# Attention with a woven-in GLU: the last two head groups alternate chunk by chunk, so that output projections run during the last six blocks

## Chip, cores, metric

One core of a Trainium2 chip (trn2). The metric is device time of the whole program in microseconds, the median of several executions. Every execution also reports the mean granted TensorE clock of the core (1.0 is full speed).

Profiles are of single executions, so a span in a profile differs a little from the median of the runs, and is 1.7 us shorter than the time of the same execution.

## The reference

```python
x = A_x                                    # 1 x 2048 x 640, bf16
xn = layernorm(x)
qkv = (xn @ wqkv) -> q, k, v               # 32 heads of 20
o = softmax(q k^T / sqrt(20)) v            # 2048 x 2048 scores for each head
s = o @ wo                                 # 640 x 640
h = sigmoid(xn @ w_gate) * (xn @ w_up)     # 640 x 1728
g = silu(h @ w_down)
out = x + s * g
```

## The kernel before

The 32 heads are 8 groups of 4, the 2048 queries 4 chunks of 512, so attention is 32 blocks (group g, chunk c). For each block 64 tiles of scores (128 keys x 512 queries, one head) are made by TensorE. ScalarE takes the exponential of most, VectorE of the others (an integer conversion `iv` for each tile and three passes `pb` for four tiles); TensorE multiplies with the values (PV) into one accumulator bank `oacc`. The block is then divided by its row sums: through DRAM and GpSimd for most blocks (`norm_a`, `norm_b`), on chip with transposes for the last two. All other matmuls (GLU, values, keys, projections; "M work") are items that are woven in.

The order of instructions on TensorE, ScalarE and VectorE is computed when the program is built: a loop steps a clock of its own, with assumed durations, and at each step places what is ready. Parts (`...` marks what is left out):

```python
URGENT, ROUNDS, HOLD, SLACK, LEAD, LAG, D_LAST, D_LAST_END = 0.25, 4, 0.15, 0.2, 40.0, 0.0, 20, 8
D_ORD, M_ORD, WAIT3, FALL, M_END = 1, 0, 0.4, 1, 1.5
# ... blocks in the order g * 4 + c; the projection of chunk c (8 items of 5 matmuls) needs block (7, c)
# the projection of chunk 2 also needs one extra matmul for each item, from the block divided on chip

# the last block: division on chip, and the last projection, all but group 7's part, as a "prefill"
chain = [("DVE", 0.60, e_on), ("PE", 1.52, e_tr), ("DVE", 0.75, e_scale), ("PE", 0.42, e_back), ("DVE", 0.45, e_o)]
fill = [(t4 - 2, 0.2133, lambda t4=t4, kd=kd: early(mains[t4], t4, slice(0, 512), kd))
        for t4 in range(4) for kd in range(t_l + 1)]           # 20 matmuls of 512 columns
fill += [(2, 0.07, lambda ...: early(rest[...], t4, slice(512, D), kd, t4 == 0)) ...]   # 20 of 128 columns

def tail_steps():
    for _, _, f in fill:      # what is left of the prefill
        f()
    ...                       # group 7's part (late_mm), evacuation, residual, store

total = sum(x.work for x in items + glu_items if x.need is None)
def due():                    # how much M work should be placed by now
    return total * min(1.0, progress() / (NBLK - M_END))

# one step of the issue loop, TensorE's part
if full and pv_ok:
    nxt = "PV"
elif can_f and (margin < URGENT or (...)):    # a score buffer is free and ScalarE soon runs dry
    nxt = "F"
elif ...
if nxt == "F":
    ...
    jobs = claim_act(want, ...)
    if jobs or d_new is not None:
        ...                                    # place score matmuls
    elif pv_ok:
        nxt = "PV"
    elif m_ok:
        nxt = "M"
if nxt == "M":
    ...
elif nxt is None and fill and can_fill(fill[0][0]):
    fill.pop(0)[2]()                           # place a matmul of the prefill
elif nxt == "PV":
    ...
while chain or items or glu_items or ...       # (the loop's condition)
...
tail_steps()
```

## Time and profile before

| | before |
|---|---|
| median of the first runs | 841.25 us (839.08 to 841.6) |
| span of the profile | 839.8 us |
| last exponential ends | 812.7 us |
| from there to the end (the tail) | 27.1 us |
| exponential tiles on VectorE, of 2048 | 471 |

Busy time by stretch, kernel before. The columns are the stretch and its length, then busy time and number of instructions of each engine, the granted clock, the DMA share and GB/s:

```profile
core 0: us, PE busy (x) PEld busy (x) DVE busy (x) ACT busy (x) POOL busy (x), PEclk, DMA share, GB/s
795.00:812.70 17.70, 17.26 (x160) 6.67 (x158) 17.06 (x29) 17.69 (x21) 6.08 (x7) 1.00 0.54 169
812.70:831.20 18.50, 18.41 (x114) 8.44 (x111) 10.04 (x21) 0.00 (x0) 4.08 (x5) 1.00 0.39 124
831.20:839.80 8.60, 0.00 (x0) 0.00 (x0) 4.11 (x6) 0.00 (x0) 3.82 (x3) 0.70 0.22 78
```

In attention all three engines are nearly full; in the second row ScalarE has no work and TensorE has no idle time (18.41 of 18.50 us).

The timeline of the tail, kernel before; columns are start, duration, engine, line, operation, output and inputs, and how many were merged:

```profile
808.73 3.96 ACT L80 ACTIVATE pt<-scA 128x1024 bf16<-128x1024 f32 x4
...
814.72 0.68 DVE L985 COPY on<-oacc 128x512 f32<-128x512 f32 x1
...
817.46 0.39 PE L998 MATMUL tp<-ident,onq 128*80 128x128 bf16 x4
...
818.23 0.41 DVE L1002 COPY o<-tp 80x512 bf16<-80x512 bf16 x1
...
822.66 0.31 PE L765 MATMUL bk<-wo_l,oL 80*128 80x320 bf16 x1
...
823.03 2.42 PE L976 MATMUL scA<-wo,oU 128*128 128x512 bf16 x9
...
825.38 4.60 PE L976 MATMUL bk<-wo,oU 128*128 128x512 bf16 x30
...
829.91 0.40 PE L980 MATMUL bk<-wo_l,o 80*128 80x128 bf16 x4
...
830.34 0.69 DVE L1020 SCALAR_TENSOR_TENSOR hT<-bk,wd 128x512 f32<-128x512 f32 x1 [5.02 <-PE bk L980]
```

The division of the last block (accumulator copy L985, transposes L989, L998, copy L1002) is done at 818.6 us. TensorE is then still in chunk 2's projection (L765, to 823.0). Then come the prefill (L976, 823.0 to 829.9) and the last matmuls (L980).

```profile
L1194 DVE TENSOR_SCALAR iv<-bk 128x512 int16<-128x512 f32 x471 | 318.6, 682 | 31.7 <-PE bk L860 30.2
```

### The profile page before, as it was taken

To read this page: it belongs to the slowest core of one execution; us is meant where nothing else is said; L and a number is where in the kernel's file an instruction comes from. 1 tells how busy PE (TensorE), PEld (TensorE's weight loads), DVE (VectorE), ACT (ScalarE), POOL (GpSimd) and SP (SyncE) were. 2 spreads that over 40 slices of the span, in tenths; PEclk is the share of its full clock that TensorE was granted. 3 is DMA by queue.
4 is the path that set the end of the run, shared out by engine and by line. 5 is a ranking of instruction groups with operands and counts; after the bars stand their busy time and mean duration, and the time that the engine had idled before them with its cause. 6 is when DMAs were issued, how large, how long until landed. Compare 5 with 4: busy or idle time off the path is not lost.

```text
span 839.8 us, 16932 instructions
## 1 busy us (share of the span) xinstructions
PE 788.4 (94%) x6354; PEld 278.5 (33%) x6411; DVE 765.4 (91%) x1194; ACT 796.0 (95%) x1003; POOL 77.5 (9%) x84
## 2 busy tenths in 40 slices
PE   4799999999999999999999999999999999999995
PEld 2432323333333323333333233333233322333342
DVE  7789899999899998998999999999998988999994
ACT  7799999999999999999999999999999999999970
POOL 5000000000000001000000000000000000002333
PEclk9999999999999999999999999999999999999998
DMA  5711212123222132213121232131311223111642
GB/s 154 205 51 50 60 51 49 47 57 82 72 62 63 43 85 69 68 44 82 52 61 53 68 85 67 45 92 49 109 65 46 66 71 78 28 47 57 193 147 91
DMA packets 92979, 62.21 MB, mean 74 GB/s; under 512 B 34648, under 2 KB 86408, under 8 KB 92896
## 3 DMA queue, kind: packets, MB, share of 16 engines
q1 hardware_dynamic: 92608, 60.79, 25.7%
q8 instruction: 50, 0.82, 0.4%
q10 hardware_dynamic: 288, 0.33, 0.1%
q14 instruction: 33, 0.27, 0.1%
HBM read 46.24 MB, written 12.39 MB: 70 GB/s over the span
## 4 chain that ended last, share of the span: by engine, by line
ACT 49%; PE 28%; DVE 13%; issue 6%; DMA 2%; SPq 1%; POOL 0%; POOLq 0%; ACTq 0%; DVEq 0%
ACT pt L80 44%; PE scA L860 8%; PE oacc L897 5%; DVE iv L1194 5%; PE bk L679 4%; PE bk L641 3%; ACT tnh L80 3%; DVE pb L951 2%; PE bk L765 2%; PE bk L504 2%; DVE pb L945 1%; DVE pb L948 1%; DMA ld<-on 1%; PE psk L140 1%; ACT td L80 1%
## 5 line engine op out<-in xcount | busy, mean ns | idle before, releaser
L80 ACT ACTIVATE pt<-scA 128x1024 bf16<-128x1024 f32 (+1 forms) x729 | 720.2, 1153 | 4.6 <-PE bk L860 2.9
L1194 DVE TENSOR_SCALAR iv<-bk 128x512 int16<-128x512 f32 x471 | 318.6, 682 | 31.7 <-PE bk L860 30.2
L860 PE MATMUL scA<-q,kT 32*128 32x512 bf16 x1448 | 282.6, 382 | 16.7 <-ACT pt L80 9.6
L860 PE MATMUL bk<-q,kT 32*128 32x512 bf16 x600 | 215.5, 383 | 2.0 <-DVE iv L1194 1.7
L897 PE MATMUL oacc<-pt,v 128*21 128x512 bf16 x1577 | 183.1, 382 | 0.6 <-ACT pt L80 0.3
L860 PEld LDWEIGHTS <-kT 32*128 32x128 bf16 x2048 | 88.7, 91 | 261.6 <-issue 246.8
L897 PE MATMUL oacc<-pb,v 128*21 128x512 bf16 x942 | 152.9, 382 | 1.8 <-DVE on L910 1.5
L951 DVE TENSOR_TENSOR pb<-iv,pb 128x2048 bf16<-128x2048 bf16 x118 | 146.8, 1244 | 0.8
L641 PE MATMUL bk<-xnT,wgu 128*128 128x512 bf16 x471 | 142.6, 383 | 3.6 <-issue 1.7
L927 POOL TENSOR_TENSOR on_bf<-on,rl 128x512 bf16<-128x512 f32 x30 | 43.3, 1443 | 692.7 <-DMA rl<-rd 326.0
L80 ACT ACTIVATE pt<-bk 128x512 bf16<-128x512 f32 x129 | 94.5, 733 | 4.0 <-PE bk L860 3.8
L945 DVE TENSOR_SCALAR pb<-iv 128x2048 int16<-128x2048 int16 x118 | 86.3, 731 | 2.5
L679 PE MATMUL bk<-wd,hT 128*128 128x320 bf16 x448 | 86.9, 302 | 1.2 <-DVE iv L1194 0.7
L948 DVE TENSOR_SCALAR pb<-iv 128x2048 int16<-128x2048 int16 x118 | 82.6, 700 | 0.0
L897 PEld LDWEIGHTS <-v 128*21 128x21 bf16 x2519 | 50.4, 90 | 92.2 <-issue 69.4
L641 PEld LDWEIGHTS <-wgu 128*128 128x128 bf16 x520 | 37.1, 97 | 66.2 <-issue 50.4
L679 PEld LDWEIGHTS <-hT 128*128 128x128 bf16 x448 | 34.4, 97 | 48.4 <-issue 39.4
L504 PE MATMUL bk<-xnT,wu 128*120 128x512 bf16 x160 | 49.3, 399 | 0.4 <-DVE iv L1194 0.3
L80 ACT ACTIVATE tnh<-bk 128x512 bf16<-128x512 f32 (+1 forms) x56 | 41.6, 742 | 0.1
L649 DVE SCALAR_TENSOR_TENSOR hT<-tnh,bk 128x512 bf16<-128x512 bf16 x52 | 35.3, 680 | 5.9 <-PE bk L641 5.2
L612 PE MATMUL bk<-wv,xnT 128*128 128x160 bf16 x280 | 29.2, 234 | 0.7 <-ACT pt L80 0.6
L612 PEld LDWEIGHTS <-xnT 128*128 128x128 bf16 x280 | 18.6, 98 | 14.4 <-issue 14.1
(116 smaller groups left out, 381.3 us busy)
## 6 DMA issues: line engine op xcount, KB each, us to landing
wgu<-in_B_w_gate_dram SPq DMA_DIRECT2D x24, 320.0 KB
wgu<-in_B_w_up_dram SPq DMA_DIRECT2D x24, 320.0 KB
rl<-rd SPq DMA_DIRECT2D x120, 64.0 KB
gq_dram<-gqs SPq DMA_DIRECT2D x32, 160.0 KB
xnT<-gq_dram SPq DMA_DIRECT2D x12, 320.0 KB
xt<-in_A_x_dram SPq DMA_DIRECT2D x16, 160.0 KB
wd<-in_B_w_down_dram SPq DMA_DIRECT2D x1, 2080.0 KB
oU<-on_bf SPq DMA_DIRECT2D x104, 20.0 KB
```

The costliest lines, as they stand in the source:

```text
L80: return nc.scalar.add_instruction(mybir.InstActivation(func=func, name=nc.get_next_instruction_name(), engine=ENG.Activation, ins=[nc.sca ...
L504: nc.tensor.matmul(st["ps"][0:UC, :], lhsT=wus[u][:, kd, i, :], rhs=xnT[:, c, kd, :], start=(kd == 0), stop=(kd == KD - 1))
L612: nc.tensor.matmul(st["ps"][:, i * 2 * GC:(i + 1) * 2 * GC], lhsT=xn_tok(tts[i], kd), rhs=wvs[pr][:, kd, :], start=(kd == 0), stop=(kd == ...
L641: nc.tensor.matmul(st[key][0:fs, :], lhsT=w[:, i, kd, ko * P:ko * P + fs], rhs=xnT[:, c, kd, :], start=(kd == 0), stop=(kd == KD - 1))
L679: nc.tensor.matmul(st["ps"][:, 0:HD], lhsT=hT[0:fsz[kf], kf, t4 * P:(t4 + 1) * P], rhs=wd[0:fsz[kf], kf, h * HD:(h + 1) * HD], start=(kf = ...
L860: nc.tensor.matmul(dst, lhsT=kTs[(b // NQC) % 2][32 * j:32 * j + 32, kt * P:(kt + 1) * P], rhs=qts[b % 3][32 * j:32 * j + 32, :], start=Tr ...
L897: nc.tensor.matmul(oacc[32 * j:32 * j + DH + 1, :], lhsT=lhsT, rhs=u["src"], start=first, stop=last, tile_position=(0, 32 * j), skip_group ...
L927: nc.gpsimd.tensor_tensor(out=on_bf, in0=on, in1=rl, op=ALU.mult)
L945: nc.vector.tensor_scalar(out=pb[:, 0, :, :].bitcast(I16), in0=iv, scalar1=0x7F80, scalar2=1, op0=ALU.bitwise_and, op1=ALU.bitwise_or)
L948: nc.vector.tensor_scalar(out=pb[:, 1, :, :].bitcast(I16), in0=iv, scalar1=0x007F, scalar2=0x3F00, op0=ALU.bitwise_and, op1=ALU.bitwise_or)
L951: nc.vector.tensor_tensor(out=pb[:, 1, :, :], in0=iv.bitcast(BF16), in1=pb[:, 1, :, :], op=ALU.mult)
L1194: nc.vector.tensor_scalar(out=d["iv"][:, j, :], in0=bank[bk], scalar1=B_OFF, scalar2=0.0, op0=ALU.add, op1=ALU.max)
```

## The change

The intent: take chunk 2's projection out of the tail. Blocks of groups 6 and 7 alternate, (6,0), (7,0), (6,1), (7,1) and so on, so when chunks 0, 1 and 2 are complete, six, four and two blocks are still to come instead of three, two and one, and only block (7,3) has to be divided on chip. The pacing counts the projections (`total`) and spreads M work nearly to the end (`M_END`). The prefill is split so that the parts that need group 6's last block come last.

```diff
-D_ORD, M_ORD, WAIT3, FALL, M_END = 1, 0, 0.4, 1, 1.5
+D_ORD, M_ORD, WAIT3, FALL, M_END = 1, 0, 0.4, 1, 0.3
...
+    PAIR = NBLK - 2 * NQC
+    def gc(b):
+        if b < PAIR:
+            return divmod(b, NQC)
+        return NG - 2 + (b - PAIR) % 2, (b - PAIR) // 2
...  (divmod(b, NQC) becomes gc(b) everywhere; mk_div and the extra matmuls of chunk 2 are gone)
-        if b >= NBLK - NQC and c > 0:
+        if g == NG - 2 and c > 0:
             for t4 in range(4):
                 for h in range(2):
                     mk.append(lambda at, t=4 * (c - 1) + t4, h=h: [mk_out(t, h, at)])
...
+    fill = []
+    for kds in (range(t_l - 1), range(t_l - 1, t_l + 1)):
+        fill += [... the 512-column parts for kd in kds]
+        fill += [... the 128-column parts for kd in kds]
...
-        total = sum(x.work for x in items + glu_items if x.need is None)
+        total = sum(x.work for x in items + glu_items)
```

More of the change, by code (lines that the diff above doesn't have):

```diff
@@ L427, with blk @@
     NBLK = NG * NQC
+    PAIR = NBLK - 2 * NQC
[3 more added lines that the diff above has]
+        return NG - 2 + (b - PAIR) % 2, (b - PAIR) // 2
+    def blk(g, c):
+        return g * NQC + c if g < NG - 2 else PAIR + 2 * c + g - (NG - 2)
     NJOB = GH * TT
@@ L471, in mk_q @@
     def mk_q(b, at):
-        g, c = divmod(b, NQC)
+        g, c = gc(b)
         st = {}
@@ L596, in load_q @@
     def load_q(b):
-        g, c = divmod(b, NQC)
+        g, c = gc(b)
         cs = slice(c * QC, (c + 1) * QC)
@@ L698 @@
     wo_l = late.tile([GC, D], BF16, name="wo_l")
-    oL = []
     def div_scale(tps):
@@ L708, in div_scale @@
         return onq
-    def mk_div(on, b):
-        st = {}
-        def a1():
-            st["t"] = misc_ps()
-        def a2():
-            st["u"] = misc_ps().bitcast(BF16)
-        def tr(i):
-            nc.tensor.transpose(out=st["t"][:, i * P:(i + 1) * P], in_=on[:, i * P:(i + 1) * P], identity=ident_f)
-        def sc():
-            st["q"] = div_scale(st["t"])
-        def back():
-            for i in range(4):
-                nc.tensor.transpose(out=st["u"][0:GC, i * P:(i + 1) * P], in_=st["q"][:, i, :], identity=ident)
-        def ev():
-            o = w2.tile([GC, QC], BF16, tag="on_bf", bufs=2, name="oL")
-            nc.vector.tensor_copy(out=o, in_=st["u"][0:GC, 0:QC])
-            oL.append(o)
-        return [Item([("PE", a1, [(0.22, lambda i=i: tr(i)) for i in range(4)]),
-                      ("DVE", 0.75, sc, "free", mark("div", b))], 0.0, pre=[("on", b)]),
-                Item([("PE", a2, [(0.30, back)]),
-                      ("DVE", 0.40, ev, "free", lambda t: o_at.__setitem__(b, t))], 0.0, pre=[("div", b)])]
     def load_out(tt):
@@ L754, in alloc @@
             st["ps"] = misc_ps()
-        split = tt // 4 == NQC - 2
         def mm(kd):
             hs = slice(h * HD, (h + 1) * HD)
-            if kd == KD:
-                lhsT, rhs = oL[0][:, tt % 4 * P:(tt % 4 + 1) * P], wo_l[:, hs]
-            else:
-                rows = o_l if split and kd == t_l else P
-                lhsT, rhs = oU[0:rows, kd, tt * P:(tt + 1) * P], wo[0:rows, kd, hs]
-            nc.tensor.matmul(st["ps"][:, 0:HD], lhsT=lhsT, rhs=rhs, start=(kd == 0),
-                             stop=(kd == KD - 1 + split))
+            nc.tensor.matmul(st["ps"][:, 0:HD], lhsT=oU[:, kd, tt * P:(tt + 1) * P], rhs=wo[:, kd, hs],
+                             start=(kd == 0), stop=(kd == KD - 1))
         def ev():
@@ L777, in ev @@
                 nc.sync.dma_start(out=out2[tt * P:(tt + 1) * P, :], in_=xr)
-        return Item([("PE", alloc, [(0.136, lambda kd=kd: mm(kd)) for kd in range(KD + split)]),
-                     ("DVE", 0.40, ev, "free", mark("o", tt, h))], at, need=(NG - 1) * NQC + tt // 4,
+        return Item([("PE", alloc, [(0.136, lambda kd=kd: mm(kd)) for kd in range(KD)]),
+                     ("DVE", 0.40, ev, "free", mark("o", tt, h))], at, need=blk(NG - 1, tt // 4),
                     pre=[("d", tt // 4, t4, i) for t4 in range(4) for i in range(2)] + [("h", 2, kf) for kf in range(NFT)] + (
@@ L794 @@
     for b in range(NBLK):
-        g, c = divmod(b, NQC)
+        g, c = gc(b)
         mk = []
@@ L859, in score_mm @@
     def score_mm(dst, b, kt, j):
-        nc.tensor.matmul(dst, lhsT=kTs[(b // NQC) % 2][32 * j:32 * j + 32, kt * P:(kt + 1) * P],
+        nc.tensor.matmul(dst, lhsT=kTs[gc(b)[0] % 2][32 * j:32 * j + 32, kt * P:(kt + 1) * P],
                          rhs=qts[b % 3][32 * j:32 * j + 32, :], start=True, stop=True, tile_position=(32 * j, 0))
@@ L879, in pv_pick @@
         for u in pv_q[j]:
-            if u["b"] == pv_block[0] and u["ready"] <= now and v_at.get((u["b"] // NQC // 2, u["kt"]), 1e9) <= now:
+            if u["b"] == pv_block[0] and u["ready"] <= now and v_at.get((gc(u["b"])[0] // 2, u["kt"]), 1e9) <= now:
                 return u
@@ L889, in pv_emit @@
             b, kt, j, k = u["b"], u["kt"], u["j"], u["k"]
-            pr, go = divmod(b // NQC, 2)
+            pr, go = divmod(gc(b)[0], 2)
             pv_q[j].remove(u)
@@ L917, in norm_b @@
     def norm_b(b, on, lt):
-        g, c = divmod(b, NQC)
+        g, c = gc(b)
         rt = w2.tile([P, GH * QC // P], FP32, tag="rt", bufs=2, name="rt")
@@ L1004 @@
     chain = [("DVE", 0.60, e_on), ("PE", 1.52, e_tr), ("DVE", 0.75, e_scale), ("PE", 0.42, e_back), ("DVE", 0.45, e_o)]
-    fill = [(t4 - 2, 0.2133, lambda t4=t4, kd=kd: early(mains[t4], t4, slice(0, 512), kd))
-            for t4 in range(4) for kd in range(t_l + 1)]
-    fill += [(2, 0.07, lambda t4=t4, kd=kd: early(rest[:, t4 * EX:(t4 + 1) * EX], t4, slice(512, D), kd, t4 == 0))
-             for t4 in range(4) for kd in range(t_l + 1)]
+    fill = []
+    for kds in (range(t_l - 1), range(t_l - 1, t_l + 1)):
+        fill += [(t4 - 2, 0.2133, lambda t4=t4, kd=kd: early(mains[t4], t4, slice(0, 512), kd))
+                 for t4 in range(4) for kd in kds]
+        fill += [(2, 0.07, lambda t4=t4, kd=kd: early(rest[:, t4 * EX:(t4 + 1) * EX], t4, slice(512, D), kd, t4 == 0))
+                 for t4 in range(4) for kd in kds]
     def tail_steps():
@@ L1104 @@
                 blk_loaded = bb
-                g, c = divmod(bb, NQC)
+                g, c = gc(bb)
                 if c == 0 and g + 1 < PG:
@@ L1125 @@
             if q_next < NBLK and base() >= q_next - 2:
-                us_ = [u for u, _, _, _ in spans(q_next // NQC)]
-                if all(ev_at.get(("qD", u, q_next % NQC), 1e9) <= now and ev_at.get(("bD", u), 1e9) <= now for u in us_) \
-                        and q_next // NQC in k_at:
+                qg, qc = gc(q_next)
+                us_ = [u for u, _, _, _ in spans(qg)]
+                if all(ev_at.get(("qD", u, qc), 1e9) <= now and ev_at.get(("bD", u), 1e9) <= now for u in us_) \
+                        and qg in k_at:
                     load_q(q_next)
-                    q_at[q_next] = max(now + 5.0, k_at[q_next // NQC])
+                    q_at[q_next] = max(now + 5.0, k_at[qg])
                     q_next += 1
@@ L1144 @@
                     oacc_at[0] = now + T_ON + EL
-                    if norm_pending[0] == NBLK - 2:
-                        on = w2.tile([P, QC], FP32, tag="on", bufs=2, name="on")
-                        nc.vector.tensor_copy(out=on, in_=oacc)
-                        items[0:0] = mk_div(on, norm_pending[0])
-                        ev_at[("on", norm_pending[0])] = free["DVE"] + EL
-                    else:
-                        timed.append((free["DVE"] + 6.5, norm_pending[0]) + norm_a(norm_pending[0]))
+                    timed.append((free["DVE"] + 6.5, norm_pending[0]) + norm_a(norm_pending[0]))
                     norm_pending = None
```

## The prediction

> **What bounds the kernel now.** Profile of 839.8 us (timed median 841.25), from the busy times by stretch:
>
> - 90 to 812.5 us: attention with the GLU woven in. ScalarE, which does most exponentials, is busy about 716 of 722 us (99%), VectorE 90 to 96%. Scores run at 258 to 270 per 100 us whatever other matmuls TensorE has. TensorE's busy share (97%) says little: the Trainium skill, "Perfetto Trace Analysis", Per-engine timelines, says that matmul ends are estimated. In the waits of 90 to 812 us TensorE's own waits are small, ScalarE's total 5 us, and VectorE waits 26 us for score matmuls. ScalarE sets the pace.
> - 812.7 to 839.8 us: a tail of 27 us without exponentials. In the timeline: last PV 814.5; on-chip division of the last block 814.7 to 818.6; but TensorE works through chunk 2's projection (all 48 matmuls after 813.3) until 823.0, then the prefilled projection of chunk 3, 40 matmuls, 823.0 to 829.9, then 9.9 us of last matmuls, evacuation and store. So the tail is bound by TensorE's queue, not by the division.
>
> **What the change does.** In the old order block (7,2) is the last but one, so chunk 2's projection can start only in the tail. In the new order it is the third from last (accumulator copies lie 24.3 us apart): its copy falls near 766 us. The ordinary division took 13 us to the GpSimd product and the projections started 23 to 25 us after the copy, so chunk 2's can run from about 789 us and be done before 812, as chunk 1's were in 794 to 811.
>
> Removed from the tail: 813.3 to 823.0 except PV and transposes, about 8.3 us of TensorE. Removed altogether: one on-chip division (VectorE 1.2 us, eight transposes) and eight extra 80-row matmuls. The prefill can start when the last exponentials leave their banks.
>
> New tail: from 811.3, 17 PV matmuls (1.4 us with switches), transposes 1.1 us, prefill 7.0 us (5 matmuls of 512 columns per 1.28 us, i.e. 256 ns each), so it ends near 821 instead of 829.9: 8.8 us saved. The division chain, ending 818.6, stays just under it.
>
> Added to the attention stage: 8 us of TensorE and eight evacuations of 0.48 us on VectorE, less the 1.2 us of division: 2.7 us, about two exponential tiles (iv 0.68 plus passes 0.67 us each) go to ScalarE at 0.47 us. I expect attention to end 1 to 1.5 us later.
>
> **Predicted: 833.8 us** (841.25 − 8.8 + 1.3), range 829.5 to 838.5. Faster by over 2%: 0.04; within 2%: 0.94; slower: 0.02.
>
> **Right, if** after it the last exponential ends at 812 to 816; no chunk-2 projection stands in the tail; prefill begins about 1 us after the last score and ends near 821 to 823; the tail from last exponential to end is 18 to 19.5 us, with the last 9.9 us unchanged; scores per 20 us remain 52 to 54 from 680 us on.
>
> **Wrong, if** the projections of chunks 0 and 1 (from about 690 and 740) push the GLU's last products so late that the tail's loads of the gated values hold the evacuation; if their loads, in order on one DMA queue, hold up GLU weights or the softmax round trips; if keys of group 7 arrive late for block 25; or if the denser TensorE stream starves VectorE so that ScalarE takes more tiles (attention ending 3 us or more later).

## More of the kernel before

Who made VectorE wait in the last blocks, kernel before (from 690 to 820 us; us in total, times, longest), and the group of VectorE's conversions (count, busy us, mean ns, idle before them):

```profile
DVE iv L1194 <- PE bk L860: 4.1, 7, 2.0
```

The start of attention, kernel before (columns of the first table):

```profile
30.00:35.00 5.00, 2.31 (x26) 1.29 (x24) 3.45 (x7) 2.42 (x5) 0.00 (x0) 1.00 1.12 325
35.00:40.00 5.00, 4.46 (x49) 2.61 (x48) 3.79 (x7) 5.00 (x8) 0.00 (x0) 1.00 1.07 362
40.00:45.00 5.00, 4.87 (x47) 1.62 (x40) 4.12 (x8) 5.00 (x8) 0.00 (x0) 1.00 0.81 181
```

## The result, and the profile after

| | before | after |
|---|---|---|
| median of the runs on the same chip | 840.77 us (4 runs) | 841.99 us (4 runs) |
| ratio | | 1.0005, 95% interval 0.9983 to 1.0028 |
| granted clock of the four runs | | 0.987, 0.991, 0.991, 0.988 |
| span of the profile | 839.8 us | 841.0 us |
| last exponential ends | 812.7 us | 818.7 us |
| tail | 27.1 us | 22.3 us |
| tiles on VectorE | 471 | 464 |

Ratios here and below are the mean time of one kernel's fast runs over that of the other's in the same rounds, so they are not quite the ratios of the medians.

No gain: 4.8 us came off the tail and 6.0 us were added to attention. The busy times by stretch, kernel after (same columns):

```profile
795.00:818.70 23.70, 22.75 (x207) 7.89 (x200) 22.59 (x37) 23.53 (x28) 9.17 (x9) 1.00 0.45 147
818.70:832.30 13.60, 11.24 (x60) 5.08 (x60) 3.15 (x6) 0.00 (x0) 0.00 (x0) 0.87 0.03 7
832.30:841.00 8.70, 0.49 (x3) 0.00 (x0) 4.59 (x7) 0.00 (x0) 3.82 (x3) 0.56 0.21 75
```

In the second row TensorE now has idle time (11.24 busy of 13.60 us), and its clock was down to 0.87. The timeline of the tail, kernel after:

```profile
817.12 1.58 ACT L80 ACTIVATE pt<-scA 128x1024 bf16<-128x1024 f32 x2
...
819.70 0.40 PE L871 MATMUL oacc<-pb,v 128*21 128x512 bf16 x4 [0.57 <-DVE pb L925]
...
820.14 0.69 DVE L959 COPY on<-oacc 128x512 f32<-128x512 f32 x1 [0.50 <-PE oacc L871]
...
820.89 0.66 PE L963 MATMUL scA<-ident_f,on 128*128 128x128 f32 x4 [0.79 <-DVE on L959]
...
822.49 0.42 PE L972 MATMUL tp<-ident,onq 128*80 128x128 bf16 x4 [0.94 <-DVE onq L715]
...
822.74 2.35 PE L950 MATMUL scA<-wo,oU 128*128 128x512 bf16 x6
823.00 0.42 DVE L976 COPY o<-tp 80x512 bf16<-80x512 bf16 x1 [0.56 <-PE tp L972]
...
824.88 2.97 PE L950 MATMUL bk<-wo,oU 128*128 128x512 bf16 x18
...
831.53 0.40 PE L954 MATMUL bk<-wo_l,o 80*128 80x128 bf16 x4
...
831.96 0.69 DVE L996 SCALAR_TENSOR_TENSOR hT<-bk,wd 128x512 f32<-128x512 f32 x1 [8.54 <-PE bk L954]
```

No projection of chunk 2 is left in the tail: that step worked. But the prefill (L950) starts at 822.74 us, four microseconds after the last exponential and directly after the second transposes of the division (L972), not "about 1 us after the last score". Before L963 and L972 TensorE waited for VectorE (0.79 and 0.94 us in brackets). And the prefill lasts from 822.7 to 831.5, 8.8 us instead of 7.0.

VectorE's waits in the last blocks and its conversions, kernel after:

```profile
DVE iv L1165 <- PE bk L834: 8.2, 13, 1.0
```

```profile
L1165 DVE TENSOR_SCALAR iv<-bk 128x512 int16<-128x512 f32 x464 | 313.0, 681 | 43.0 <-PE bk L834 42.1
```

Its waits for score matmuls have doubled in the last blocks (4.1 to 8.2 us), over the whole run its idle time before conversions rose from 31.7 to 43.0 us, and it converted seven tiles fewer.

The start of attention, kernel after (same columns as before):

```profile
30.00:35.00 5.00, 2.25 (x25) 1.17 (x22) 3.45 (x7) 2.42 (x5) 0.00 (x0) 0.97 1.12 328
35.00:40.00 5.00, 5.00 (x32) 2.58 (x29) 2.87 (x5) 4.14 (x5) 0.00 (x0) 0.50 1.08 356
40.00:45.00 5.00, 5.00 (x36) 1.61 (x34) 3.94 (x6) 3.79 (x5) 0.00 (x0) 0.51 0.55 128
```

From 35 to 45 us TensorE ran at half clock, and ScalarE was busy only 4.14 and 3.79 of 5 us. In the kernel before the clock was 1.00 there, though TensorE had been idle as much just before (2.31 us busy from 30 to 35 us, against 2.25). Nothing in the change touches this place on purpose.

So there are three things to explain: the place of the prefill, the half clocks, and the longer attention.

### The profile page after: what moved, and what is told of

The parts are those of the page before. It is cut to its first block, busy times and chain, and to the rows that moved or that the text cites. A ratio compares the mean times of both kernels' runs of the same rounds, so it can differ in the third digit from the quotient of the medians.

```text
span 841.0 us, 16951 instructions
## 1 busy us (share of the span) xinstructions
PE 793.8 (94%) x6388; PEld 278.7 (33%) x6388; DVE 756.5 (90%) x1174; ACT 799.7 (95%) x1007; POOL 84.3 (10%) x90
## 4 chain that ended last, share of the span: by engine, by line
ACT 39%; PE 36%; DVE 16%; issue 5%; DMA 2%; SPq 1%; POOL 0%; POOLq 0%; ACTq 0%; DVEq 0%
ACT pt L80 36%; PE scA L834 11%; PE oacc L871 8%; PE bk L651 6%; DVE iv L1165 6%; PE bk L689 5%; DVE pb L925 3%; DVE pb L919 2%; DVE pb L922 2%; PE bk L514 1%; ACT tnh L80 1%; PE bk L622 1%; PE psk L140 1%; DVE hT L659 1%; PE bk L834 1%
## 5 line engine op out<-in xcount | busy, mean ns | idle before, releaser
L80 ACT ACTIVATE pt<-scA 128x1024 bf16<-128x1024 f32 x728 | 718.9, 1147 | 5.1 <-PE bk L834 2.9
L1165 DVE TENSOR_SCALAR iv<-bk 128x512 int16<-128x512 f32 x464 | 313.0, 681 | 43.0 <-PE bk L834 42.1
L834 PE MATMUL bk<-q,kT 32*128 32x512 bf16 x598 | 211.0, 385 | 1.3 <-DVE iv L1165 1.3
L871 PE MATMUL oacc<-pb,v 128*21 128x512 bf16 x928 | 148.3, 382 | 1.7 <-DVE pb L925 1.2
L925 DVE TENSOR_TENSOR pb<-iv,pb 128x2048 bf16<-128x2048 bf16 x116 | 149.2, 1286 | 0.7
L651 PE MATMUL bk<-xnT,wgu 128*128 128x512 bf16 x520 | 147.0, 382 | 2.4 <-DVE iv L1165 0.7
L80 ACT ACTIVATE pt<-bk 128x512 bf16<-128x512 f32 x134 | 96.6, 721 | 6.1 <-PE bk L834 5.7
L919 DVE TENSOR_SCALAR pb<-iv 128x2048 int16<-128x2048 int16 x116 | 84.4, 728 | 2.8 <-PE oacc L871 0.3
L922 DVE TENSOR_SCALAR pb<-iv 128x2048 int16<-128x2048 int16 x116 | 81.1, 699 | 0.0
L622 PE MATMUL bk<-wv,xnT 128*128 128x160 bf16 x280 | 31.2, 245 | 0.9 <-ACT pt L80 0.6
L749 POOL TENSOR_TENSOR xnT<-otmp,xnT 128x320 bf16<-128x320 f32 x24 | 23.1, 970 | 49.5 <-DVE otmp L746 45.6
```

What stands on the lines that cost most here:

```text
L80: return nc.scalar.add_instruction(mybir.InstActivation(func=func, name=nc.get_next_instruction_name(), engine=ENG.Activation, ins=[nc.sca ...
L651: nc.tensor.matmul(st[key][0:fs, :], lhsT=w[:, i, kd, ko * P:ko * P + fs], rhs=xnT[:, c, kd, :], start=(kd == 0), stop=(kd == KD - 1))
L834: nc.tensor.matmul(dst, lhsT=kTs[gc(b)[0] % 2][32 * j:32 * j + 32, kt * P:(kt + 1) * P], rhs=qts[b % 3][32 * j:32 * j + 32, :], start=True ...
L871: nc.tensor.matmul(oacc[32 * j:32 * j + DH + 1, :], lhsT=lhsT, rhs=u["src"], start=first, stop=last, tile_position=(0, 32 * j), skip_group ...
L919: nc.vector.tensor_scalar(out=pb[:, 0, :, :].bitcast(I16), in0=iv, scalar1=0x7F80, scalar2=1, op0=ALU.bitwise_and, op1=ALU.bitwise_or)
L922: nc.vector.tensor_scalar(out=pb[:, 1, :, :].bitcast(I16), in0=iv, scalar1=0x007F, scalar2=0x3F00, op0=ALU.bitwise_and, op1=ALU.bitwise_or)
```

## Experiments

My theory after the result had three parts. A: the prefill is late because of its place in TensorE's program. In the issue loop, when all scores are placed and both score buffers are free, `nxt` becomes "F", nothing can be placed, and `nxt` stays "F": the branch for the prefill, which wants `nxt is None`, is never reached, and all 40 matmuls are issued by `tail_steps` after the division. (Counting at build time confirms it: 40 of 40 were left for `tail_steps`, in the kernel before too, where it cost little, because chunk 2's projection filled the division's waits.) L: the moved work lengthens attention. C: the half clocks are chance. The rivals: B, the prefill waited for data (the outputs of block (6,3), whose stores were issued from 817.3 to 821.0 us); O, alternating two groups is itself slower; and that the start's clock belongs to the changed program.

Medians in the table are of each kernel's own rounds; "before" is the unchanged kernel in the same rounds on the same chip.

| kernel | median us | before | ratio (95%) | last exponential, profile | tail |
|---|---|---|---|---|---|
| e1 prefill reached | 836.67 | 841.33 | 0.9945 (0.9921 to 0.9970) | 814.4 | 18.4 |
| e2 without chunk 2 | 839.26 | 841.33 | 0.9980 (0.9957 to 1.0003) | 815.7 | 24.1 |
| e3 order only | 840.62 | 841.33 | 0.9993 (0.9972 to 1.0014) | 812.7 | 25.4 |
| e4 pacing to the end | 836.18 | 841.33 | 0.9943 (0.9919 to 0.9967) | 812.9 | 21.0 |
| e5 after, again | 840.09 | 842.64 | 0.9971 (0.9950 to 0.9992) | 818.6 | 22.3 |
| e6 before, busy start | 839.51 | 842.64 | 0.9973 (0.9947 to 0.9999) | 811.8 | 27.1 |
| e7 after, busy start | 839.62 | 842.64 | 0.9961 (0.9944 to 0.9977) | 814.2 | 23.8 |
| e8 combined | 833.31 | 842.64 | 0.9886 (0.9866 to 0.9905) | 811.4 | 20.2 |
| e9 after, busy start and gaps | 838.31 | 841.70 | 0.9954 (0.9939 to 0.9969) | 815.4 | 20.9 |
| e10 order only, busy start | 839.46 | 841.70 | 0.9967 (0.9952 to 0.9982) | 813.1 | 24.6 |
| e11 prefill reached, busy start | 835.84 | 841.70 | 0.9925 (0.9909 to 0.9940) | 815.6 | 18.5 |
| e12 before, busy start by identity | 840.74 | 842.91 | 0.9978 (0.9957 to 0.9998) | 812.3 | 27.1 |

All gave the right result but e2, which leaves out rows on purpose. By a limit of 2% each of them is the same as the kernel before; an interval that leaves out 1.0 shows a smaller difference, and those of e2 and e3 don't. e1 to e8 ran on chip 13, e9 to e11 on chip 7, e12 on chip 10: small differences between medians of different rounds are to be read with care (e6 and e12, nearly the same program, differ by 1.2 us).

### e1: let the issue loop reach the prefill

```diff
                     elif m_ok:
                         nxt = "M"
+                    else:
+                        nxt = None
                 if nxt == "M":
```

> The changed kernel with one line more: when no score is left to place, the issue loop goes on to the prefill of the last projection instead of idling; 12 of the 40 prefill matmuls then stand before the end of the on-chip division in TensorE's program. Theory A (the prefill was late because of its place in the program): attention ends where it did (last exponential near 818 us in the profile), the prefill starts before 821 us instead of 822.7, the clock stays full, the last prefill matmul ends 3 to 4 us earlier, near 828, and the time falls by 3 to 5 us against the changed kernel (842.0), to 837 to 839. Theory B (the prefill waited for data, the outputs of block (6,3) landing near 821 to 823 us): TensorE stalls at the first prefill matmul, the division ends later, and the time is the same or worse (842 or more).

Measured: 836.67 us against 841.99 for the change alone (other rounds) and 841.33 for the kernel before. The timeline of e1:

```profile
812.83 1.57 ACT L80 ACTIVATE pt<-scA 128x1024 bf16<-128x1024 f32 x2
...
814.76 0.39 PE L950 MATMUL scA<-wo,oU 128*128 128x512 bf16 x1
...
815.83 0.69 DVE L959 COPY on<-oacc 128x512 f32<-128x512 f32 x1 [0.50 <-PE oacc L871]
...
823.32 0.40 PE L954 MATMUL bk<-wo_l,o 80*128 80x128 bf16 x4
```

The prefill began at 814.8 us, 0.4 us after the last exponential, with no wait; the division did not suffer (accumulator copy 815.8, last copy 818.9). The tail was 18.4 us, which is what the prediction had for the change (18 to 19.5). Theory A holds and B falls: the data were there. The Trainium skill, "TensorE: Matmul & The Clock Gate", Part 2, says that matmuls stay in program order and that only weight loads are pulled ahead; the timelines agree, in the changed kernel the gaps of 0.79 and 0.94 us stood before 40 matmuls, of which at least 12 had nothing to wait for: e1 places these 12 ahead of the division's end.

This run also says something about the start. Up to 811 us e1 is the same program as the change, and yet its last exponential came at 814.4, not 818.7. The start of attention in e1:

```profile
35.00:40.00 5.00, 4.53 (x51) 2.52 (x48) 4.26 (x7) 5.00 (x7) 0.00 (x0) 1.00 1.08 351
40.00:45.00 5.00, 4.92 (x43) 1.63 (x40) 4.12 (x7) 5.00 (x7) 0.00 (x0) 1.00 0.69 161
```

Same instructions, clock 1.00. So the half clock is not a property of the program, and attention ended 4.3 us later in the profiled run that had 10 us of it (818.7 against 814.4). These are two single profiles: against the four profiles of this program with a full clock at the start, told under e10 (814.2 to 815.6), it is 3.1 to 4.5 us.

### e2 and e3: without chunk 2's projection, and the new order alone

e2 leaves chunk 2's eight items out; e3 holds them until the last score is placed and keeps them out of the pacing:

```diff
 e2:
-                    mk.append(lambda at, t=4 * (c - 1) + t4, h=h: [mk_out(t, h, at)])
+                    if c < 3:
+                        mk.append(lambda at, t=4 * (c - 1) + t4, h=h: [mk_out(t, h, at)])
 e3:
-            items += f(b + 0.9 * i / len(mk))
+            items += f(NBLK - 0.015 if b == NBLK - 2 and i >= len(mk) - 8 else b + 0.9 * i / len(mk))
-        total = sum(x.work for x in items + glu_items)
+        total = sum(x.work for x in items + glu_items if x.at < NBLK - 0.1)
```

> Wrong result on purpose: the changed kernel without the eight projection items of chunk 2 (its 512 rows are not written). Theory L: last exponential 2 to 4 us earlier than in the changed kernel, tail unchanged at 22.3 us, total 838 to 840. Theory O: last exponential within 1 us of the changed kernel's 818.7, total 841 to 842.

> The changed block order, but chunk 2's eight projection items are held until the last score is placed, and the pacing doesn't count them. Theory L (the moved TensorE and VectorE work lengthens attention): the last exponential ends 2 to 4 us earlier than in the changed kernel, 814 to 816 us in the profile, with about 470 tiles on VectorE as before the change; the tail is 9 us longer again, and the total 842 to 845. Theory O (alternating two head groups is itself slower, by key and query loads or the softmax round trips): the last exponential stays at 818 us or later, and the total is 846 or more.

Measured: e3's last exponential was at 812.7, as in the kernel before, though the blocks alternate and though its clock was 0.66 from 35 to 40 us. Theory O, in the form that the order alone costs the 6 us, falls. But two other expectations of theory L failed as well: the end was 1 to 3 us earlier than the 814 to 816 expected, and VectorE took 465 tiles, not about 470. The waits for scores in the last blocks were even longer than in the change, 10.2 us against 8.2. So neither the lost tiles nor these waits come from chunk 2's projection. e2 had the same order of instructions up to there and ended attention at 815.7, but its start ran at half clock from 35 to 40 us; this muddied what it was meant to show, and I repeated e3 with the start fixed (e10). My expectation for e3's total (842 to 845) was wrong: 840.6. Its tail was 25.4 us, only 3.1 longer than the 22.3 of the change, although all of chunk 2's projection was in it. That is the point that the prediction missed: in a tail that waits for a division, eight projection items cost 3 us, not 8, because most of them run in its gaps. (The 22.3 contain a prefill partly at half clock; against e9 below, with a full clock, e10's tail is 3.7 us longer, 24.6 against 20.9.) Taking them out uncovers the gaps.

### e4: pacing to the very end

```diff
-... M_END = 1, 0, 0.4, 1, 0.3
+... M_END = 1, 0, 0.4, 1, 0.0
```

> The changed kernel with its pacing constant M_END 0.0 instead of 0.3: the other matmuls are spread to the very end of attention, 1% thinner. If attention's length hangs on how densely other matmuls are paced, the last exponential ends about 3 us earlier (the kernel's own issue arithmetic says 2.9) and the total is 838 to 840, if the last GLU products don't come too late. If the pacing is not what lengthened attention: 841 to 843.

Measured: 836.18, better than expected; last exponential 812.9, although this run had half clock at the start too (0.70 from 35 to 40 us). VectorE took 472 tiles and waited less (30.7 us idle before conversions, against 43.0). So the added attention time is not a fixed price of the moved work. It should not be read as a trend: in the loop's own clock (an estimate of the program, not a measurement) the last score is placed at 778.9 with M_END 0.3, at 775.4 with 0.0, but at 779.4 with 0.05 and 778.0 with 0.1; in the kernel before it is 775.6, in e3 775.5. Small changes of the pacing reshuffle the whole order and move the end by a few microseconds.

### e5: the changed kernel again

No edit.

> The changed kernel, unaltered, once more and in more rounds. Its four first runs had a granted clock of 0.987 to 0.991, and the profiled one ran 10 us at half clock between 34 and 45 us, which the first experiment, the same program up to 811 us, did not; its last exponential came 4.3 us earlier. If that is chance (the half clock comes and goes between runs of any of these kernels), further runs scatter from 837 to 843 with a median of 839 to 840.5, slower ones with a lower clock. If it belongs to the changed program, the median is 842 again and no run has a clock above 0.992.

Measured: 840.09 against 842.64, six runs of 837.8 to 842.6 with clocks from 0.989 to 0.995. As expected under chance: the change is not 842 by nature; the one run with a clock of 0.995 took 837.8. In the 40 runs of the kernel before that these rounds contain, 22 had a clock of 0.993 or less and a mean of 843.2 us, 18 had 0.994 or more and a mean of 841.0. By these clocks the half clock visits both kernels, but no profile of the kernel before caught it at the start.

### e6, e7 and e12: keep TensorE busy at the start

```diff
+            d = psP.tile([P, KD, P], BF16, tag="tp", bufs=4, name="tp")
+            def busy(n):
+                for i in range(n):
+                    nc.tensor.transpose(out=d[:, i % KD, :], in_=xns[TT - 1][:, i % KD * P:(i % KD + 1) * P],
+                                        identity=ident)      # e12: in_=ident
+            busy(22)
             q_bound(pq[0], 0, pq[1])
+            busy(12)
```

> The kernel before, with 34 idle transposes in TensorE's stream around the last bound product of the start (30 to 33 us), where it waits for VectorE. If the half clock after 34 us comes from TensorE's idle time there, no run has it: clock in the profile 1.00 from 33 to 60 us, granted clock 0.996 to 0.997 in every run, time 839.5 to 840.5 with a scatter under 1.5 us instead of 840.2 to 843.6. If it does not come from that gap, clock and scatter stay as they were.

> The changed kernel with the same 34 transposes. With the chance of the start taken away, what remains of the change is its attention (1.7 us longer by the profiles without half clock) and its tail (4.8 us shorter where the prefill ran at half clock, about 6.5 where it did not): 835.5 to 838, that is 2 to 4.5 us below the kernel before with the same transposes. If the change gains nothing apart from the clock of the start, both are within 1 us of each other.

> The kernel before with 34 idle transposes as in the earlier experiment, but of the identity matrix instead of the normalised input. In the earlier one the transposes read tiles whose place the big weight loads take over, and so the loads began 5 us later (DMA share 0.12 instead of 1.12 from 30 to 35 us): activity of TensorE and a later burst of loads were changed together. Here the loads stay at 30 us. If it is TensorE's activity that keeps the clock, the clock is 1.00 from 33 to 60 us, the runs lie at 839 to 840.5 with a granted clock of 0.995 to 0.997; if it was the later burst, about half of the runs have 0.990 to 0.993 again and the median is 841 to 842.

Measured. e6 (kernel before): 839.51, five runs of 838.9 to 840.6 with clocks of 0.995 to 0.997, and one of 845.83 with 0.989, which I cannot explain. e7 (the change): 839.62, six runs of 838.8 to 840.3. In e6 and e7 the transposes also delayed the big weight loads by 5 us, so e12 repeats e6 without that: loads at 30 us as ever, and the clock stayed up there:

```profile
30.00:35.00 5.00, 4.07 (x59) 3.12 (x56) 3.45 (x7) 2.34 (x5) 0.00 (x0) 1.00 1.11 326
35.00:40.00 5.00, 4.54 (x48) 2.50 (x47) 3.95 (x7) 5.00 (x7) 0.00 (x0) 1.00 1.08 361
```

e12's six runs had clocks of 0.995 to 0.997 and 840.1 to 841.3 us, while the unchanged kernel in the same rounds went from 839.9 to 845.2; the median, 840.74, is a little above the 839 to 840.5 expected. It is TensorE's activity at the start that decides, not the later loads. The Trainium skill, "TensorE: Matmul & The Clock Gate", Part 1, describes a monitor that watches a free-running window of about 3.4 us and halves the clock after an idle one, so that the same kernel does differently from run to run. The traces agree as to the chance between runs (0.50 and 1.00 in 35:40) and the length: every half clock that ended inside a program here lasted 3.4, 6.8 or 10.2 us. They do not agree that the window has to be idle: in the 3.41 us before the change's half clock (31.27 to 34.68) TensorE was busy 1.77 us. Within attention, e12's profile has 3.4 us at half clock from 789.9 us, after a stretch of 3.41 us with a single gap of 0.72 us. That the place of the window decides between two runs with the same gaps fits, but is not shown here.

With the start's chance taken away the change is worth nothing measurable: 839.6 against 839.5, in the same rounds. My expectation for e7 (835.5 to 838) was too low by about 2 us, because in that profile the whole first half of the prefill ran at half clock and attention was 2.4 us longer, not 1.7. The prefill in e7:

```profile
818.76 2.77 PE L958 MATMUL scA<-wo,oU 128*128 128x512 bf16 x6
821.32 3.52 PE L958 MATMUL bk<-wo,oU 128*128 128x512 bf16 x18
...
828.51 0.40 PE L962 MATMUL bk<-wo_l,o 80*128 80x128 bf16 x4
```

It took from 818.76 to 828.51, 9.75 us.

### e9: keep TensorE busy in the division's gaps

The prefill stays behind the division; seven matmuls of no use are put into the gaps, on top of e7:

```diff
     def e_tr():
+        dummy(3)                  # 128x128 weights, 512 columns, into a bank that the prefill overwrites
         for i in range(4):
             nc.tensor.transpose(...)
+        dummy(4)
```

> The changed kernel with the 34 transposes at the start, its order of instructions otherwise untouched, plus seven idle matmuls of 512 columns in the two gaps of the on-chip division (three before its first transposes, four after), so that TensorE's clock isn't taken down before the prefill, which stays behind the division. If the half clock of the prefill is a separate cost beside its place, the 40 prefill matmuls take 7.0 to 7.3 us instead of 9.8, the granted clock is 1.00 from 815 to 830 us, and the time is 2 to 2.8 us below the 839.6 of the same kernel without them: 836.8 to 837.6. If the clock follows something else, the prefill stays at 9 to 10 us and the time at 839 to 840.

Measured: 838.31, 1.3 us below e7, less than the 2 to 2.8 expected. The prefill in e9:

```profile
816.99 0.82 PE L971 MATMUL scA<-wo,ident 128*128 128x512 bf16 x3
...
818.35 1.03 PE L971 MATMUL scA<-wo,ident 128*128 128x512 bf16 x4
...
819.71 1.46 PE L958 MATMUL scA<-wo,oU 128*128 128x512 bf16 x6
821.01 2.13 PE L958 MATMUL bk<-wo,oU 128*128 128x512 bf16 x18
...
826.81 0.40 PE L962 MATMUL bk<-wo_l,o 80*128 80x128 bf16 x4
```

From 819.71 to 826.81, 7.1 us at clock 1.00 instead of 9.75: in the profile all that was expected. By the medians it is less; e7's other runs may not all have been as cold (clocks from 0.991 to 0.995), but they have no profile, and e7 ran on another chip in other rounds, where the ratios to the kernel before (0.9961 and 0.9954) differ by less than their intervals. So the clock's cost is shown in the profiles, and not by the medians. This splits the loss in the tail: the clock is one part, the place another. e9's first six matmuls, 819.71 to 821.01, are 217 ns each; e7's first six, 818.76 to 821.32, are 427 ns each.

### e10: the order alone, with a busy start

> The alternating order with chunk 2's projection held to the end (as in the second experiment), with the 34 transposes. Free of the start's clock, the last exponential is near 811.5 us (order costs nothing: 811.8 in the kernel before with the same transposes) against 814.2 with chunk 2's projection in attention; total 837.5 to 839. If the 2.4 us longer attention came from the order of blocks, it stays at 814 us here too.

Measured: 839.46, total a little above the expected range; last exponential 813.1 (expected near 811.5). The profiles with full clock at the start end attention at 811.8, 812.3 and 812.7 in the kernel before (mean 812.3), at 814.2, 814.4, 815.4 and 815.6 with the change (mean 814.9, e7, e1, e9, e11, all the same program up to there but for the transposes), and at 813.1 here. So of 2.6 us, about 1.8 go with the moved work and 0.8 might go with the order, but the same program scatters by 1.4 us, and 0.8 is not shown. Nor is the moved work parted from the pacing: e10 also takes it out of `total`, and the order of instructions differs from about 62 us on. VectorE took 465 tiles here, almost as few as in the change.

### e11: the prefill reached, with a busy start

On top of e7: e1's two lines, and the parts of the prefill that lie in plain banks placed first, so that they need not wait for the last exponential's buffer.

```diff
-        for t4 in range(4) for kd in kds]       # main parts
+        for t4 in (2, 3) for kd in kds]
         ... 128-column parts ...
+        fill += [... for t4 in (0, 1) for kd in kds]
```

> The changed kernel with the transposes and with the prefill reached by the issue loop, parts in plain banks first (21 of the 40 prefill matmuls before the division's end), pacing unaltered (M_END 0.3). Against 839.6 with the transposes alone: prefill ends 5 to 6 us earlier by its place and its clock together, so 833.5 to 835; the last exponential stays at 814.2. The difference to the kernel that also paces to the very end (833.3) is then what the pacing is worth once the prefill is in place: 0 to 2 us.

Measured: 835.84 (835.4 to 836.0), 3.8 us below e7 (other rounds) and 2.5 below e9 (same rounds; the slowest run of e11 is 1.0 us below the fastest of e9); a little above the range expected, as attention ended 1.4 us later than in e7. TensorE's timeline, prefill (L958) around the division (L971 and the product that writes tp):

```profile
815.32 0.60 PE L958 MATMUL bk<-wo,oU 128*128 128x512 bf16 x2
...
817.20 0.99 PE L958 MATMUL bk<-wo,oU 128*128 128x512 bf16 x6
818.06 0.66 PE L971 MATMUL scA<-ident_f,on 128*128 128x128 f32 x4
818.55 0.67 PE L958 MATMUL bk<-wo,oU 128*128 128x128 bf16 x9
...
819.66 0.42 PE L980 MATMUL tp<-ident,onq 128*80 128x128 bf16 x4
...
824.62 0.40 PE L962 MATMUL bk<-wo_l,o 80*128 80x128 bf16 x4
```

The prefill fills every gap; the last matmuls start at 824.6 us, and the tail is 18.5 us.

### e8: all together

e7 with e11's prefill and e4's pacing.

> The changed kernel with the 34 transposes, the prefill reached by the issue loop with the bank-held parts first, and pacing to the very end (M_END 0.0). If the three effects add: 842 less 3 (start), less 4 to 5 (prefill), less 2 to 3 (pacing), that is 830 to 833; if the prefill's gain and the pacing's are the same gain twice, 834 to 836.

Measured: 833.31 us, five runs within 0.9 us, ratio 0.9886; 0.3 us above the range expected if the effects add. This is a version that beats both kernels, the kernel before by 1.1% and the change by about 0.8% (e5 in the same rounds, 840.09). Its conversions on VectorE, against the lines shown above:

```profile
L1175 DVE TENSOR_SCALAR iv<-bk 128x512 int16<-128x512 f32 x472 | 319.9, 684 | 29.8 <-PE bk L842 27.7 <-PE scA L842 0.2
```

The distance to e11 is what pacing gave here (M_END is the only difference): 2.5 us by medians of different rounds, somewhat more than the 0 to 2 expected. In the profile attention ended at 811.4, against 814.2 to 815.6.

## Why the prediction was wrong

The class was right: within 2%, held to be 0.94 likely. The range was not: 841.99 lies outside 829.5 to 838.5, and where 7.5 us were expected, between nothing and 2.5 us came.

- **Bound of the tail: wrongly concluded.** "So the tail is bound by TensorE's queue, not by the division" was true of the kernel before, but by a margin that the change itself removes. The step that failed is "**The prefill can start when the last exponentials leave their banks**" and the sum behind it, "so it ends near 821 instead of 829.9: 8.8 us saved". On an engine that takes its instructions in order, the prefill can start where it stands in the program, and it stands behind the division. The issue loop's branch for it was in the code that I had, and I did not check that it is ever reached. In the change it began at 822.74, 4.0 us after the last exponential, and ended at 831.5. The tail shrank by 4.8 us (e5: the same; e7: 3.3). e1 and e11, which only move the prefill, have the predicted tail (18.4 and 18.5 us, predicted 18 to 19.5).
- **A cost that the prediction did not have: the clock.** Gaps before the prefill let its first part run at half clock. The prefill took 9.75 us in e7 and 7.1 us in e9, so 2.65 us in the profiles (by the medians, of different chips, 1.3 us, not clear of noise); moving the prefill into the gaps is worth 2.5 us more (e11 against e9).
- **Attention later by "1 to 1.5 us": mis-sized, and the mechanism is not borne out.** With the start's chance removed it is 2.6 us in the profiles (812.3 to 814.9). I had two tiles go from VectorE to ScalarE, for the moved work; the change has seven (464 instead of 471). But e3 and e10, without the moved work in attention, have 465 tiles and longer waits for scores, and end at 812.7 and 813.1. And e4 and e8 have the moved work and 472 tiles, and end at 812.9 and 811.4. So the tiles go with the pacing (e4 differs from the change in M_END alone), the moved work has no fixed price, and how the 2.6 us come about stays open.
- **The 6.0 us of the first comparison** were 3.1 to 4.5 us of chance at the start, as e1 and the other profiles of the same program show, and the rest the above. The profiled run of the change happened to have it, that of the kernel before did not.
- **Right:** no projection of chunk 2 in the tail; the end part from the first evacuation to the store nearly unchanged (before 830.34 to 839.8, after 831.96 to 841.0, 9.4 and 9.0 us); the dangers named with loads, keys and late GLU products did not come true (ScalarE's wait for scores in the last blocks was under 1 us).

Worked out for a calm start: tail 27.1 to 23.8 (e6 to e7) gives back 3.3 us; attention takes 2.4 us (811.8 to 814.2) in the same two profiles; 0.9 us is left, and by the medians of e6 and e7 nothing (839.5 and 839.6).

Open: why one run of e6 took 845.8 us with a granted clock of 0.989; whether the alternating order costs the 0.8 us that e10 hints at; why the pacing answers so unevenly, and with it what lengthens attention by 2.6 us; and why the same gaps at the start halve the clock in one run and not in the next.

## What to carry to other kernels

Work that stands in a tail is only worth what it holds up: before you count its removal, ask what will wait there next, and where each following instruction stands in its engine's program; a matmul that waits for nothing still waits for everything issued before it. If an order is computed by a program, count how often each of its branches was taken before trusting that it is used. And when two profiles differ at a place that the change doesn't touch, look at the granted clock by stretch and repeat the run before explaining it.

## What the Trainium skill lacked or had wrong

- "TensorE: Matmul & The Clock Gate", "Why this matters for your kernels", advises no idle gaps over about 3 us. Here no single gap was that long, and the clock was halved all the same: before the start's half clock the gaps were 1.3, 0.8 and 0.6 us (TensorE busy 2.25 of 5 us), before the prefill 0.57, 0.79 and 0.94 us. (Part 1 of the page does tell of a kernel whose clock went up and down after frequent short idle times, without their lengths.) Such gaps don't always do it: the kernel before had 1.3, 0.8 and 0.6 us at the start too, at clock 1.00. 22 of 40 runs of one kernel had a mean clock of 0.993 or less; 10 us of half clock at the start cost 3.1 to 4.5 us of 841 in the profiles.
- The same page, Part 4, says that a transpose doesn't count as TensorE being busy in the same way. Transposes by the identity, which the trace records as ordinary matmuls, did keep the clock up at the start here: 34 of them, 56 ns apart, six of six runs at 0.995 to 0.997 (e12). The trace doesn't tell whether the page's transpose mode was on for them.
- "TensorEngine Tiling (Array Packing)", Key Properties, says that a change of tiling mode drains the engine, without a figure. Here four 512-column matmuls with 128 rows and one with 48 rows took 1.28 us (kernel before, prefill), against 5 x 217 ns = 1.09 us for the pure series of e9: about 0.2 us for going to 48 rows and back. That it is the drain, and not the weight load or the 48 rows themselves, is not shown.
